# Attention among the experts' matmuls: a unit in two groups of steps, and single steps where attention is alone

## The chip, the cores and the metric

The kernel runs on one core of one Trainium2 chip. The metric is the device time of one execution in microseconds (us). It was 879.05 us in the median of three runs (876.48 to 881.49).

A core has five engines, each with its own queue of instructions: TensorE (PE in the profile; its weight loads are PEld), VectorE (DVE), ScalarE (ACT), GpSimd (POOL) and SyncE (SP). SP computes nothing here and issues most of the DMA transfers. An engine works through its queue in order, and an instruction waits until what it needs has been done by the other engines.

## The reference

Sigmoid attention over 8 batches, 12 heads, 448 rows and head size 64, and behind it a mixture of 8 experts on the 3584 x 768 result:

```python
scores = scale * np.matmul(q, k.transpose(0, 1, 3, 2)) - np.log(S)
attn = 1.0 / (1.0 + np.exp(-scores))
attn_out = np.matmul(attn, v)
...
logits = x @ w_gate
expert_idx = np.argmax(logits, axis=1)
...
for e in range(E):
    mask = expert_idx == e
    xe = x[mask]
    h = np.maximum(xe @ w1[e], 0.0)
    out[mask] = gate_w[mask, None] * (h @ w2[e])
```

Each row goes to one expert only, and gate_w is the softmax probability of that expert. There is no row maximum or sum in the attention, so a block of keys can be worked through by itself.

## The kernel before

**Stages.** First attention runs alone on TensorE. Then attention and the experts run side by side: for each batch of 448 rows the expert that most of its rows chose is applied to all of them. In a tail the rows that chose another expert are gathered into work items and done again. The change touches the first two stages.

**Attention.** Heads go in pairs, 48 pairs g in all (6 per batch); two pairs make a unit u, and the keys of a unit are cut into ST = 7 steps of 64 keys. So there are N_ST = 168 steps, s = 7u + i. For a step, `scores(s)` (L515) gives for each of the two pairs a tile of 128 x 448 scores in PSUM (tag "sc", a ring of 4 tiles, so two steps; the gate's small products take turns in the same ring), followed by the sigmoid on ScalarE into a tile `at` in SBUF (`squash`, L507; a ring of 8, so four steps). `weighted(s)` (L526) multiplies the sigmoids by v and sums over the 7 steps of the unit in one PSUM tile per pair (tag "av", a ring of 2, so one unit). After the last step of a unit the sums are read three times: a copy xh by ScalarE (L543), the rest xl = sum - xh by VectorE (L544) and a transpose into xt by VectorE (L400). All these products are 64 x 64 matmuls in float32, four of them side by side on the quarters of the array; each shows as two records in the trace, so one step of scores, or of value sums, is 8 records.

**Experts.** `moe(b, wts)` (L192) is a generator that yields after every matmul of 128 x 128 by 448 columns. A batch has 288: eight blocks of 18 for the first layer (L208) and six of 24 for the second (L229). Their PSUM tiles have the tag "moe", a ring of 2. Weights arrive as raw float32 tiles (`wst`, a ring of 5) and are split into two parts: a cast on ScalarE (L143) and a subtraction on GpSimd (L144). `wts.ahead(n)` emits loads and splits up to part n. A block of the first layer ends with a Relu on ScalarE (L213) and a VectorE operation (L214).

**Order.** In these stages the order of the instructions on each engine is the program's (`manual_schedule`). The generator `attention()` (L560) walks s from 0 to 178 and yields twice per s; at each yield the loop at L639 puts 7 expert matmuls (MIX) into the program, from s = START = 36 on. Between the yields come, by i = s mod 7, transposes of the next unit's k and q on VectorE and loads (`READY`, L553: `turn`, `load_pair`, `load_values`), and the parts of the gate of a batch (`gate_a` to `gate_e`, at fixed s behind the batch's last unit). `load_pair` issues 8 DMAs per pair on SP (L445); `token_rows` stores xt to x_tok with four DMAs on SP (L408); `load_regs` reads the chosen expert on SP, and the loads of `wst` follow on SP.

Attention products stand at every even s: first the value sums of all steps before s (before s - 1 as long as s < START), stopping at the end of a unit, and then the scores of s and s + 1. With s < 36 there are no expert matmuls, and these groups follow one another on TensorE.

Of the kernel before, what the change touches and what calls it, by code (L numbers as in the profile page):

```python
# [10 lines left out]
F32 = mybir.dt.float32  # L11
# [8 lines left out]
P = 128  # L20
# [5 lines left out]
def tile_sigmoid_attention_top1_moe(  # L26
# [41 lines left out]
    ps_moe = ctx.enter_context(tc.tile_pool(name="ps_moe", bufs=2, space=bass.MemoryType.PSUM))  # L68
# [317 lines left out]
    def load_regs(b):  # L386
        ri = gate_out[b]
        regs[b] = nc.sync.value_load(ri[0:1, 0:1], min_val=0, max_val=E - 1)
# [5 lines left out]
    def token_block(g, pv):  # L394

        b, t = divmod(g, NP)
        n, t = divmod(t, KH)
        if t == 0:
            xts[b, n] = xtpool.tile([P, S // 32, KH, 32], F32, tag="xt", bufs=2, name=f"xt_{b}_{n}")
        nc.vector.transpose(xts[b, n][:, :, t, :], pv.rearrange("p (j s) -> p j s", s=32))  # L400
        if t == KH - 1:
            turned.append((b, n))
# [18 lines left out]
    ps_av = att.enter_context(tc.tile_pool(name="ps_av", bufs=2, space=bass.MemoryType.PSUM))  # L421
# [10 lines left out]
    def quarter(g, h):  # L432

        return OWN[h if g % 2 == 0 else 1 - h]

    def load_pair(g):
        if g >= NG:
            return
        b, hp = divmod(g, NP)
        for nm, src in (("k", k), ("q", q)):  # L440
            t = apool.tile([P, S // 32, 32], F32, tag=nm + "n", bufs=4, name=f"{nm}n_{g}")
            for h in range(2):
                for f in range(D // 32):
                    a = 2 * h + f
                    nc.sync.dma_start(  # L445
                        t[32 * a : 32 * (a + 1)],
                        src[b, 2 * hp + h, :, 32 * f : 32 * (f + 1)].rearrange("(j r) s -> r j s", r=32),
                    )
            ops[g, nm + "n"] = t

    def first_pair(g):

        b, hp = divmod(g, NP)
        t = wpool.tile([P, 1024], F32, tag="wst", bufs=RAWS_AHEAD, name=f"first_{g}")
        tv = t[:PF].rearrange("p (n c h d) -> p n c h d", n=2, c=4, h=2)
        for n, src in enumerate((k, q)):
            for h in range(2):
                eng = nc.scalar if n else nc.sync
                eng.dma_start(tv[:, n, :, h], src[b, 2 * hp + h].rearrange("(p c) d -> p c d", c=4))
        ops[g, "first"] = t  # L460

    def first_turn(g):

        t = ops.pop((g, "first"))
        for n, nm in enumerate("kq"):
            ps = score_tile(f"first_{g}_{nm}")
            for c in range(4):
                at = (4 * n + c) * P
                nc.tensor.transpose(ps[:, c * PF : (c + 1) * PF], t[:PF, at : at + P], ident[:PF, :PF])
            to = apool.tile([P, S], F32, tag=nm + "t", bufs=4, name=f"{nm}t_{g}")  # L470
            tov, psv_ = to.rearrange("d (p c) -> d c p", c=4), ps[:, :S].rearrange("d (c p) -> d c p", c=4)
            if nm == "k":
                nc.vector.tensor_copy(tov, psv_)
            else:
                nc.scalar.copy(tov, psv_)
            ops[g, nm] = to

    def load_values(g):
        if g >= NG:
            return  # L480
        b, hp = divmod(g, NP)
        eng = nc.gpsimd if g < V_POOL else nc.sync
        t = apool.tile([P, KC, D], F32, tag="vn", bufs=4, name=f"vn_{g}")
        for h in range(2):
            eng.dma_start(t[quarter(g, h)], v[b, 2 * hp + h].rearrange("(p c) d -> p c d", c=KC))
        ops[g, "v"] = t
# [9 lines left out]
    def warm_up(n):  # L496

        ps = ps_moe.tile([P, 512], F32, tag="moe", name="ps_warm")
        for _ in range(n):
            nc.tensor.matmul(ps[:, :P], ones, ones, start=True, stop=True)  # L500

    ats, psv = {}, {}

    ST = KC
    N_ST = NG // 2 * ST

    def squash(g, c, ps):  # L507
        at = apool.tile([P, S], F32, tag="at", bufs=8, name=f"at_{g}_{c}")
        nc.scalar.activation(at, ps[:, :S], AF.Sigmoid, bias=bias_s, scale=SCALE)  # L509
        ats[g, c] = at  # L510

    def score_tile(name):
        return ps_sc.tile([P, 512], F32, tag="sc", name=f"sc_{name}")

    def scores(s):  # L515
        u, c = divmod(s, ST)
        two = [2 * u + n for n in range(2)]
        pss = [score_tile(f"{g}_{c}") for g in two]
        for g, ps in zip(two, pss):
            for h in range(2):  # L520
                ks = ops[g, "k"][OWN[h]].rearrange("d (p c) -> d c p", c=KC)[:, c]
                nc.tensor.matmul(ps[quarter(g, h), :S], ks, ops[g, "q"][OWN[h]], start=True, stop=True)  # L522
        for g, ps in zip(two, pss):
            squash(g, c, ps)

    def weighted(s):  # L526
        u, c = divmod(s, ST)
        two = [2 * u + n for n in range(2)]
        for g in two:
            if c == 0:  # L530
                psv[g] = ps_av.tile([P, 512], F32, tag="av", name=f"av_{g}")
            at = ats.pop((g, c))
            for h in range(2):
                rows = quarter(g, h)
                nc.tensor.matmul(  # L535
                    psv[g][OWN[h], :S], ops[g, "v"][rows, c, :], at[rows], start=(c == 0), stop=(c == KC - 1)
                )
        if c == KC - 1:
            for g in two:
                pv = psv.pop(g)  # L540
                xh = xpool.tile([P, S], F32R, tag="xh", name=f"xh_{g}")
                xl = xpool.tile([P, S], F32R, tag="xl", name=f"xl_{g}")
                nc.scalar.copy(xh, pv[:, :S])  # L543
                nc.vector.tensor_sub(xl, pv[:, :S], xh.bitcast(F32))  # L544
                token_block(g, pv[:, :S])
                xch[divmod(g, NP)] = (xh, xl)

    WARM, V_POOL = 50, 10
    START = 36
    PB = NP // 2 * ST  # L550
    MIX = (7, 7)

# [7 lines left out]
    def attention():  # L560

        order = ExitStack()
        order.enter_context(tc.manual_schedule())
        for g in range(2):
            first_pair(g)
        warm_up(WARM)
        for g in range(2):
            first_turn(g)
            load_values(g)
        for g in (2, 3):  # L570
            load_pair(g)
        nc.gpsimd.dma_start(wg, w_gate.rearrange("(t p) e -> p t e", p=P))
        pend_gate = None
        done_av = 0
        for s in range(N_ST + 11):
            u, i = divmod(s, ST)
            if s == 6:
                setup()
            if s == START - 1:
                wts.ahead(2)  # L580
            if s % 2 == 0:


                while done_av < min(s - (s < START), N_ST):
                    weighted(done_av)
                    done_av += 1
                    if done_av % ST == 0:
                        break
                for n in range(s, min(s + 2, N_ST)):
                    scores(n)  # L590
            yield s, MIX[0]
            if i in READY and s < N_ST:
                READY[i](u)
            gb = s - PB
            if gb >= 0:
                b, r = divmod(gb, PB)
                r -= 3 if b == 0 else 2
                at = ("a", "b", None, "c", "l", None, "d", None, "e")
                what = at[r] if 0 <= r < len(at) else None
                if what == "a":  # L600
                    gate_a(b)
                elif what == "b":
                    pend_gate = gate_b(b)
                elif what == "c":
                    pend_gate = gate_c(b, *pend_gate)
                    gate_out[b] = pend_gate[0]
                elif what == "l":
                    load_regs(b)
                    if b == 0:
                        wts.ahead(0)  # L610
                elif what == "d":
                    gate_d(b, *pend_gate)
                elif what == "e":
                    gate_e(b)
            yield s, MIX[1]
            if s % 2 == 0:
                while turned:
                    token_rows(*turned.pop(0))
        order.close()
# [19 lines left out]
    for s, n in attention():  # L639
        if s >= START:  # L640
            more(n)
# [304 lines left out]
```

## Time and profile before

| | |
|---|---|
| median of three runs | 879.05 us (876.48 to 881.49) |
| the profiled execution | 879.22 us, span 877.2 us |
| granted TensorE clock, mean | 0.994 |
| first attention product | 10.75 us |
| first expert matmul | 80.37 us |
| the last attention product is done | 701.2 us |
| HBM traffic | 97.55 MB read, 24.64 MB written |

The span reaches from the first to the last instruction of one profiled execution; the 2 us beside it lie around the program. In a row of the timeline stand the start and the length in us, the engine, the line of the kernel, the operation, output<-input, sizes and, behind x, how many instructions were merged into the row. In brackets stands how long the engine was idle before, and what released it. Rows that overlap run side by side.

### The profile page before, as it was taken

What the parts mean: (1) busy time and instruction counts of PE and PEld (TensorE: products, weight loads), DVE (VectorE), ACT (ScalarE), POOL (GpSimd) and SP (SyncE); (2) the same over time, 40 slices, a digit from 0 to 9 for tenths busy, and PEclk for the clock granted to TensorE, in tenths of its full rate; (3) what the DMA queues carried; (4) which work ended last, traced back from release to release, by engine and by line L of the source; (5) the groups of instructions that cost most, each with busy time, mean ns of one, the idle gap of its engine ahead of it and who ended that gap; (6) DMA issues with size and microseconds to landing.
All of it is one profiled execution on the core that took longest, in us unless ns stands there. A gap on an engine that the chain in (4) does not pass through costs nothing.

```text
span 877.2 us, 15559 instructions
## 1 busy us (share of the span) xinstructions
PE 851.8 (97%) x5612; PEld 627.8 (72%) x5612; DVE 298.2 (34%) x679; ACT 383.6 (44%) x691; POOL 410.1 (47%) x377
## 2 busy tenths in 40 slices
PE   8999999999999999999999999999999998999986
PEld 6545667677677667677667667677767687899775
DVE  2444135132332134122432135123332045426454
ACT  5766443444344444345344445255344421324444
POOL 4114234734275324834276324824285458766240
PEclk9999999999999999999999999999999999999999
DMA  8988874576457764675357654586253425556623
GB/s 146 147 146 185 178 164 116 131 163 140 98 115 148 170 141 107 148 155 142 64 138 179 158 117 100 125 190 146 57 135 111 133 52 145 146 159 192 211 65 134
DMA packets 301930, 120.61 MB, mean 137 GB/s; under 512 B 211588, under 2 KB 296660, under 8 KB 301856
## 3 DMA queue, kind: packets, MB, share of 16 engines
q1 hardware_dynamic: 292512, 104.25, 51.0%
q0 software_dynamic: 7488, 14.93, 7.0%
q8 instruction: 44, 0.72, 0.4%
q10 hardware_dynamic: 1856, 0.46, 0.3%
q14 instruction: 30, 0.25, 0.1%
HBM read 97.55 MB, written 24.64 MB: 139 GB/s over the span
## 4 chain that ended last, share of the span: by engine, by line
PE 83%; SPq 7%; issue 3%; POOL 2%; DMA 2%; DVE 1%; ACT 0%; POOLq 0%; ACTq 0%; DVEq 0%
PE ps L208 28%; PE ps L229 25%; PE av L535 12%; PE sc L522 11%; SPq L445 5%; PE ps L822 4%; PE psg L256 2%; DMA out_dram<-ob 1%; SPq L408 1%; DMA first<-in_q_dram 1%; POOL w1l L144 1%; DVE w1l_item L144 1%; POOL recs L361 0%; SPq L165 0%; POOL out_dram L244 0%
## 5 line engine op out<-in xcount | busy, mean ns | idle before, releaser
L509 ACT ACTIVATE at<-sc,bias_s 128x448 f32<-128x448 f32 x336 | 187.8, 641 | 219.6 <-PE sc L522 215.1
L144 POOL TENSOR_TENSOR w2l<-wst,w2h 128x512 fp32r<-128x512 f32 x96 | 121.6, 1291 | 172.6 <-ACT w2h L143 166.9
L144 POOL TENSOR_TENSOR w1l<-wst,w1h 128x768 fp32r<-128x768 f32 x64 | 116.8, 1840 | 130.2 <-ACT w1h L143 126.8
L535 PE MATMUL av<-at,vn 64*64 64x448 f32 x1344 | 156.4, 548 | 1.3 <-PE sc L522 0.7
L522 PE MATMUL sc<-qt,kt 64*64 64x448 f32 x1344 | 153.9, 540 | 0.0
L208 PE MATMUL ps<-xh,w1l 128*128 128x448 f32 x384 | 142.6, 371 | 5.5 <-POOL w1l L144 5.5
L229 PE MATMUL ps<-hh,w2l 128*128 128x448 f32 x384 | 143.1, 373 | 0.3 <-POOL w2l L144 0.3
L208 PE MATMUL ps<-xl,w1h 128*128 128x448 f32 x384 | 142.6, 371 | 0.0
L208 PE MATMUL ps<-xh,w1h 128*128 128x448 f32 x384 | 142.3, 371 | 0.0
L229 PE MATMUL ps<-hh,w2h 128*128 128x448 f32 x384 | 142.1, 370 | 0.0
L229 PE MATMUL ps<-hl,w2h 128*128 128x448 f32 x384 | 141.9, 370 | 0.0
L522 PEld LDWEIGHTS sc<-qt,kt 64*64 64x64 f32 x1344 | 77.8, 190 | 60.0 <-issue 51.0
L214 DVE SCALAR_TENSOR_TENSOR hl<-ps,hh 128x448 fp32r<-128x448 f32 x64 | 39.9, 624 | 209.5 <-ACT hh L213 209.5
L535 PEld LDWEIGHTS av<-at,vn 64*64 64x64 f32 x1344 | 48.4, 132 | 66.7 <-issue 51.7
L208 PEld LDWEIGHTS ps<-xh,w1l 128*128 128x128 f32 x384 | 72.6, 189 | 20.6 <-POOL w1l L144 8.6
L229 PEld LDWEIGHTS ps<-hh,w2l 128*128 128x128 f32 x384 | 74.6, 194 | 11.3 <-issue 5.8
L208 PEld LDWEIGHTS ps<-xl,w1h 128*128 128x128 f32 x384 | 72.5, 189 | 13.8 <-issue 8.0
L208 PEld LDWEIGHTS ps<-xh,w1h 128*128 128x128 f32 x384 | 72.6, 189 | 13.5 <-issue 7.2
L229 PEld LDWEIGHTS ps<-hh,w2h 128*128 128x128 f32 x384 | 74.6, 194 | 10.4 <-issue 6.5
L213 ACT ACTIVATE hh<-ps 128x448 fp32r<-128x448 f32 x64 | 35.3, 551 | 106.8 <-PE ps L208 106.8
L229 PEld LDWEIGHTS ps<-hl,w2h 128*128 128x128 f32 x384 | 74.6, 194 | 10.0 <-issue 6.5
L143 ACT CAST w2h<-wst 128x512 fp32r<-128x512 f32 x96 | 57.8, 627 | 50.2 <-PE ps L229 41.8
(150 smaller groups left out, 815.4 us busy)
## 6 DMA issues: line engine op xcount, KB each, us to landing
wst<-in_moe_w_dram SPq DMA_DIRECT2D x64, 384.0 KB
wst<-in_moe_w_dram SPq DMA_DIRECT2D x48, 512.0 KB
x_tok<-xt SPq DMA_DIRECT2D x64, 168.0 KB
out_dram<-ob POOLq DMA_DIRECT2D x96, 112.0 KB, 2.7
kn<-in_k_dram SPq DMA_DIRECT2D x184, 56.0 KB
qn<-in_q_dram SPq DMA_DIRECT2D x184, 56.0 KB
vn<-in_v_dram SPq DMA_DIRECT2D x76, 112.0 KB
w1r<-in_moe_w_dram SPq DMA_DIRECT2D x12, 512.0 KB
```

What stands on the lines that cost most here:

```text
L143: nc.scalar.copy(hi, st)
L144: eng.tensor_tensor(lo, st, hi.bitcast(F32), op=ALU.subtract)
L208: nc.tensor.matmul(ps[:, :S], a[:, ws], b_, start=(t == 0 and n == 0), stop=(t == KD - 1 and n == 2))
L213: nc.scalar.activation(hh[:, :S], ps[:, :S], AF.Relu)
L214: nc.vector.scalar_tensor_tensor(hl[:, :S], ps[:, :S], 0.0, hh[:, :S].bitcast(F32), op0=ALU.max, op1=ALU.subtract)
L229: nc.tensor.matmul(ps[:, :S], a, b_, start=(j == 0 and n == 0), stop=(j == KF - 1 and n == 2))
L256: nc.tensor.matmul(psg[: 2 * E, :S], wgs[:, t], xch[b, t][n], start=(t == 0 and n == 0), stop=(t == KD - 1 and n == 1),)
L445: nc.sync.dma_start(t[32 * a : 32 * (a + 1)], src[b, 2 * hp + h, :, 32 * f : 32 * (f + 1)].rearrange("(j r) s -> r j s", r=32),)
L509: nc.scalar.activation(at, ps[:, :S], AF.Sigmoid, bias=bias_s, scale=SCALE)
L522: nc.tensor.matmul(ps[quarter(g, h), :S], ks, ops[g, "q"][OWN[h]], start=True, stop=True)
L535: nc.tensor.matmul(psv[g][OWN[h], :S], ops[g, "v"][rows, c, :], at[rows], start=(c == 0), stop=(c == KC - 1))
L822: nc.tensor.matmul(*a, **kw)
```

## The change

Three things change in `attention()` and one in `weighted()`.

- For s < ALONE = 35 the steps go singly: the scores of s, then the value sums of s - 2.
- From s = 35 on attention products stand only at i = 0 and i = 4 of a unit. At i = 0: the scores of four steps, with the value sums of the three steps left from the unit before in between (scores, values, scores, values, scores, values, scores). At i = 4: one step of value sums first, then the scores of three steps with a step of value sums behind each.
- The value sums of units 1 and 3 (odd units, as long as attention is alone) are taken in the two PSUM tiles of the experts, tag "moe".
- `token_rows` runs at i = 1 and i = 5 instead of at every even s.

```diff
@@ weighted
         for g in two:
             if c == 0:
-                psv[g] = ps_av.tile([P, 512], F32, tag="av", name=f"av_{g}")
+                pool, tag = (ps_av, "av") if u % 2 == 0 or s >= ALONE else (ps_moe, "moe")
+                psv[g] = pool.tile([P, 512], F32, tag=tag, name=f"av_{g}")
             at = ats.pop((g, c))
...
     START = 36
+    ALONE = 35
@@ attention
         done_av = 0
+
+        def values(to):
+            nonlocal done_av
+            while done_av < min(to, N_ST):
+                weighted(done_av)
+                done_av += 1
+                yield
+
+        def steps(first, n, to):
+
+            vs = values(to)
+            for m in range(first, min(first + n, N_ST)):
+                scores(m)
+                next(vs, None)
+            for _ in vs:
+                pass
+
         for s in range(N_ST + 11):
             u, i = divmod(s, ST)
             if s == 6:
                 setup()
             if s == START - 1:
                 wts.ahead(2)
-            if s % 2 == 0:
-
-
-                while done_av < min(s - (s < START), N_ST):
-                    weighted(done_av)
-                    done_av += 1
-                    if done_av % ST == 0:
-                        break
-                for n in range(s, min(s + 2, N_ST)):
-                    scores(n)
+            if s < ALONE:
+                steps(s, 1, s - 1)
+            elif i == 0:
+                steps(s, 4, s)
+            elif i == 4:
+                for _ in zip(range(1), values(s)):
+                    pass
+                steps(s, 3, s)
             yield s, MIX[0]
...
             yield s, MIX[1]
-            if s % 2 == 0:
+            if i in (1, 5):
                 while turned:
                     token_rows(*turned.pop(0))
```

## The prediction

> **What bounds the kernel now.** I read the page first, for the engine and the chain that ended last.
>
> ```profile
> PE 851.8 (97%) x5612; PEld 627.8 (72%) x5612; DVE 298.2 (34%) x679; ACT 383.6 (44%) x691; POOL 410.1 (47%) x377
> ...
> PE 83%; SPq 7%; issue 3%; POOL 2%; DMA 2%; DVE 1%; ACT 0%; POOLq 0%; ACTq 0%; DVEq 0%
> ```
>
> TensorE (PE) is busy 97% of the span and 83% of the chain; next comes SP's issuing of loads (SPq). A share of busy time says nothing of single stages, so I cut the span at the first expert matmul (80.37 us) and behind the last attention product (701.20) and asked for busy time by stretch.
>
> ```profile
> 10.75:80.37 69.62, 67.03 (x606) 34.09 (x606) 28.07 (x73) 47.03 (x86) 12.71 (x23) 0.98 0.87 155
> 80.37:701.20 620.83, 619.93 (x4080) 444.79 (x4078) 186.45 (x453) 272.21 (x498) 297.74 (x251) 1.00 0.59 135
> 701.20:877.20 176.00, 157.24 (x867) 141.98 (x863) 80.60 (x144) 61.94 (x106) 92.47 (x82) 0.98 0.45 138
> ```
>
> The columns are length, then busy us of PE, PE's weight loads, VectorE (DVE), ScalarE (ACT) and POOL, the granted clock, the DMA share and GB/s. Three stages: attention alone, 69.6 us, with the DMA engines at 0.87; the mixed stage, 620.8 us, PE busy throughout at full clock; and a tail that the change doesn't touch. In the mixed stage only the time that PE takes per piece of work can shrink, so I read its timeline around one visit to the attention products.
>
> ```profile
> 303.18 0.36 PE L208 MATMUL ps<-xh,w1l 128*128 128x448 f32 x1
> 303.47 1.74 PE L535 MATMUL av<-at,vn 64*64 64x448 f32 x16
> 305.03 1.68 PE L522 MATMUL sc<-qt,kt 64*64 64x448 f32 x16
> 306.64 0.47 PE L208 MATMUL ps<-xh,w1h 128*128 128x448 f32 x1
> 306.95 0.36 PE L208 MATMUL ps<-xl,w1h 128*128 128x448 f32 x1
> ...
> 312.21 0.36 PE L208 MATMUL ps<-xh,w1h 128*128 128x448 f32 x1
> ```
>
> Expert matmuls start every 0.202 us (26 of them from 306.95 to 312.21). A step's scores or value sums are 8 records on four 64x64 tiles at a time. From the matmul at 303.18 to the second one behind the visit are 3.77 us. What should they be? In the stage of attention alone scores and values follow each other without a gap:
>
> ```profile
> 30.83 1.66 PE L522 MATMUL sc<-qt,kt 64*64 64x448 f32 x12
> ...
> 32.33 1.66 PE L535 MATMUL av<-at,vn 64*64 64x448 f32 x12
> ...
> 33.83 1.66 PE L522 MATMUL sc<-qt,kt 64*64 64x448 f32 x12
> ```
>
> Two steps of scores and two of values, so two changes between the kinds, take 3.00 us: 0.75 for one step of one kind. The visit then needs 4 x 0.75 + 2 x 0.20 = 3.41 us and took 3.77: **0.36 us are lost at each visit**. A larger visit, with three steps of values and two of scores, loses the same: 4.53 - 0.41 - 3.75 = 0.37.
>
> ```profile
> 284.36 0.37 PE L208 MATMUL ps<-xh,w1h 128*128 128x448 f32 x1
> 284.66 2.49 PE L535 MATMUL av<-at,vn 64*64 64x448 f32 x24
> 286.97 1.68 PE L522 MATMUL sc<-qt,kt 64*64 64x448 f32 x16
> ...
> 288.89 0.36 PE L208 MATMUL ps<-xh,w1l 128*128 128x448 f32 x1
> ```
>
> So the loss goes with the number of visits, not with the work in them. The stage's sum supports it: 1848 expert matmuls x 0.202 = 373, 263 steps x 0.75 = 197, 66 visits x 0.36 = 24 and six gates at about 3.2 (twelve matmuls and some small ones) = 19 give 613 of 620.8. PE's waits between 78 and 700 us are almost nothing:
>
> ```profile
> PE ps L208 <- POOL w1l L144: 0.6, 1, 0.6
> PE ps L229 <- POOL w2l L144: 0.3, 1, 0.3
> ```
>
> **The change, part by part.** *Fewer visits.* Before, attention enters at every even s; with expert matmuls on both sides that is s = 38 to 168, 66 visits, the last ended by this matmul:
>
> ```profile
> 701.20 0.47 PE L208 MATMUL ps<-xh,w1h 128*128 128x448 f32 x1
> ```
>
> After, it enters at i = 0 and i = 4 of a unit: s = 39, 42, 46 and on to 168, 38 visits. 28 x 0.36 = **10.1 us less**. The same number of expert matmuls stands between the same values of s, and the scores and values are the same.
>
> *What waits inside a larger visit.* Four score tiles hold two steps, so the third step of scores must wait until ScalarE has done the first's sigmoids; before, a visit had two steps and never met that.
>
> ```profile
> 90.39 2.21 ACT L509 ACTIVATE at<-sc,bias_s 128x448 f32<-128x448 f32 x4 [3.93 <-PE sc L522]
> 92.96 0.55 ACT L213 ACTIVATE hh<-ps 128x448 fp32r<-128x448 f32 x1 [0.36 <-PE ps L208]
> 93.40 0.82 ACT L143 CAST w1h<-wst 128x768 fp32r<-128x768 f32 x1
> ```
>
> Four sigmoids take 2.21 us, so 1.1 for a step, against 1.5 for PE's step with its values: ScalarE keeps up once it has begun. Scores 0 end 0.75 us into the visit, its sigmoids by about 2.2, and scores 2 are due at 3.0: 0.8 of slack. What can eat it is a Relu and a cast queued ahead (0.55 + 0.82 = 1.4), which holds the sigmoids until 1.4 to 1.6 if a block of expert matmuls ends just before the visit: still in time. Behind a waiting score stand only PE's own values and the next expert matmuls. The unit's two copies xh (about 1.0, quoted below) come before the last step's sigmoids, so ScalarE ends some 2 us behind PE; expert matmuls follow there for 56 or 42 x 0.2 us. Bounds: nothing, and 0.34 us in each of the 38 visits (a backlog of 2 us) = 13. I take 1 us, next to the rows, by which the slack holds.
>
> [...]
>
> *Attention alone, steps singly and odd units in the experts' banks.* The stage loses PE time at unit ends:
>
> ```profile
> 36.09 2.24 PE L522 MATMUL sc<-qt,kt 64*64 64x448 f32 x14
> 38.98 3.16 PE L535 MATMUL av<-at,vn 64*64 64x448 f32 x22 [0.66 <-PE sc L522]
> ```
>
> ```profile
> 37.13 0.98 ACT L543 CAST xh<-av 128x448 fp32r<-128x448 f32 x2
> ```
>
> ```profile
> 39.32 0.63 DVE L400 STREAM_TRANSPOSE xt<-av 128x448 f32<-128x448 f32 x1
> ```
>
> The next unit's values start at 38.98, as VectorE's reads of the old banks end. With other banks for odd units this wait goes. The work up to the first expert matmul is 38 steps of scores and 35 of values = 54.8 us, with the first gate's 3.4 (twelve matmuls from 54.03 to 56.5, below, and small ones) 58.2; the stage takes 69.6, so 11.4 us are lost. After, one step of scores more is done by then (35 to 38 in the first group), 59.0 us.
>
> ```profile
> 54.03 0.38 PE L256 MATMUL psg<-xh,wgs 128*16 128x448 f32 x1
> ...
> 56.29 0.37 PE L256 MATMUL psg<-xl,wgs 128*16 128x448 f32 x1
> ```
>
> How much comes back is set by what is late next, the loads. Unit 1's last turned q stands only at 21.7, and PE in its best order would want it at 19.8, so 1.9 us stay:
>
> ```profile
> 21.06 0.65 DVE L493 STREAM_TRANSPOSE qt<-qn 128x448 f32<-128x448 f32 x1 [1.38 <-DMA qn<-in_q_dram]
> ...
> 31.57 0.65 DVE L493 STREAM_TRANSPOSE qt<-qn 128x448 f32<-128x448 f32 x1 [2.14 <-DMA qn<-in_q_dram]
> ```
>
> Without further waits the first expert matmul could start at 10.75 + 59.0 + 1.9 = 71.7. But SP issues loads back to back, half a microsecond each, and the experts' first weights stand behind them:
>
> ```profile
> 30.69 1.99 SPq L445 DMA_DIRECT2D qn<-in_q_dram  x4
> 32.78 1.99 SPq L445 DMA_DIRECT2D kn<-in_k_dram  x4
> ...
> 68.86 4.11 SPq L165 DMA_DIRECT2D wst<-in_moe_w_dram  x5
> ```
>
> Nothing on SP before 67 us waits for PE, and the diff keeps the order of SP's queue there (the rows of x_tok go at i = 1, between the same loads). So the weights are issued at 68.9 again. A load lands some 2 us behind its last issue (32.68 to the transpose at 34.6 in the timeline; that of 384 KB estimated 2 to 3): 71.2.
>
> ```profile
> 78.85 1.57 ACT L143 CAST w1h<-wst 128x768 fp32r<-128x768 f32 x2
> ```
>
> These two casts now stand ahead of the sigmoids of step 35, and scores 37 and 38 wait for sigmoids 35 and 36: 71.2 + 1.57 + 2.3 + 0.2 + 0.9 = 76.2. In the trace the experts begin here:
>
> ```profile
> 80.37 0.47 PE L208 MATMUL ps<-xh,w1h 128*128 128x448 f32 x1
> ```
>
> So 80.4 - 76.2 + 0.75 (the extra step) = **4.9 us less**; bounds 0 and 80.4 - 71.7 + 0.75 = 9.4.
>
> [...] In this trace the issues are back to back, which speaks for SP.
>
> *Moves without a price.* Storing x_tok at i = 1 and 5 instead of even s puts it later behind the evictions, never ahead of a load it used to follow by more than a step; it waits less on SP, and in the mixed stage SP mostly waits for free weight buffers. Values of a unit now begin at i = 4, when the old banks have been empty for 11 us; if that cover went, the price would be the 2 to 3 us per unit seen above.
>
> *Sum.* - 10.1 + 1.0 - 4.9 = -14. The profiled execution took 879.22 us (span 877.2), next to the median of 879.05; so **865 us**, own range 862 to 869.
>
> **Rivals.** *A. Attention alone gains nothing*, since loads hold it (DMA share 0.87, SP back to back) and the casts come first: 879.2 - 10.1 + 1.0 = 870. Against it: waits at unit ends are on PE's banks. *B. SP doesn't hold it*: 879.2 - 10.1 - 9.4 + 1.0 = 861. Against it the SP rows. *C. ScalarE breaks up the larger visits*, so that the change doesn't do what it says: with 0.34 us in 19 to 38 visits, 6.5 to 13, the time is 871 to 877; the 0.8 us of slack is against it. *D. Slower: changing between scores and values costs PE time beside expert matmuls.* Before, a visit has one change, 65 in all; after, six in each, 222: 157 more. In the visit above 16 value records take 1.56 us to the scores' start instead of 1.50; at 0.06 a change this is +9, 874. If half of the 0.36 belongs to the change, it is +28 while the visits save only 5: 898. Beyond 19/157 = 0.12 us a change the kernel is slower by over 0.5%. Against it: the 3.00 us above hold two changes at no cost; for it only that alternation beside full-size matmuls isn't in the trace.
>
> **How the numbers follow.** Forecast 55%, A 15%, B 8%, C 14%, D 8%. The range 860 to 872 holds the forecast, A, B and the near half of C; 15% is left out. A measurement of this kernel tells about 0.5%, 4.4 us, from no change. Faster by more (below 874.8): forecast, A, B and half of C, 85%; within: 6 of C, 3 of D, 9%; slower: 1 of C, 5 of D, 6%.
>
> **What would show it.** In the timeline: 38 visits, each of 7 steps' halves in 5.25 + 0.36 us; first expert matmul near 76; attention's last product ending near 687; the tail as long as before. A gap before the third scores with ScalarE as releaser is C; a visit longer than 6.1 us without a wait is D; a first expert matmul at 80 is A, at 72 B. Weights that come late in the longer runs of expert matmuls (11 us instead of 6), seen as PE waiting for POOL, would make all of it wrong.

## The result and the profile after

The changed kernel takes 887.05 us (median of four runs, 887.02 to 887.83) against 878.16 for the kernel before in the same comparison: a ratio of 1.0088, 95% interval 1.0065 to 1.011. It is **slower by 0.9%**, where 865 us was forecast, with a range of 860 to 872. The profiled execution took 887.08 us with a span of 885.1. Times and ratios here and below leave out a few executions in a slow state (one of e7's six, for example, took 1441 us at a granted clock of 0.64).

The same cut into three stages, now at the first expert matmul (81.87 us) and behind the last attention product (709.17); columns as before:

```profile
11.28:81.87 70.59, 66.75 (x615) 43.34 (x614) 28.69 (x75) 51.20 (x92) 15.67 (x24) 0.94 0.84 152
81.87:709.17 627.30, 615.07 (x4072) 451.70 (x4070) 187.49 (x452) 276.34 (x491) 294.98 (x249) 0.99 0.58 134
709.17:885.10 175.93, 158.52 (x867) 143.00 (x863) 80.83 (x144) 62.01 (x106) 92.51 (x82) 0.97 0.44 137
```

The tail is as long as before (176). Attention alone ends 1.5 us later, though it then has one step of scores more behind it (0.75); this is less than executions of one program differ by, for in the profile of e5 below, whose first stage is that of the changed kernel, the experts start at 79.70. The mixed stage, where 10 us were to be saved, is 6.5 us longer. PE was busy for 619.9 of 620.8 us there; now it is idle for 12 of 627, and the granted clock has fallen to 0.99. The waits of PE, in the page's list of who waited for whom, say for what:

```profile
PE ps L229 <- POOL w2l L144: 12.2, 4, 3.6
PE ps L208 <- POOL w1l L144: 4.8, 2, 3.8
PE sc L522 <- ACT at L509: 2.5, 1, 2.5
```

The second row is the tail's (4.9 before). The first is new: four waits for the low parts of the second layer's weights, which GpSimd (POOL) makes; before it was one of 0.3. One of the four in PE's timeline:

```profile
449.02 0.37 PE L229 MATMUL ps<-hl,w2h 128*128 128x448 f32 x1
453.03 0.47 PE L229 MATMUL ps<-hh,w2l 128*128 128x448 f32 x1 [3.65 <-POOL w2l L144]
453.35 0.29 PE L381 MATMUL pg<-gm,same 128*128 128x16 f32 x2
453.49 0.60 PE L229 MATMUL ps<-hh,w2h 128*128 128x448 f32 x1
453.89 0.57 PE L229 MATMUL ps<-hl,w2h 128*128 128x448 f32 x1
...
455.75 0.57 PE L229 MATMUL ps<-hh,w2h 128*128 128x448 f32 x1
456.26 1.35 PE L536 MATMUL av<-at,vn 64*64 64x448 f32 x8
```

4.0 us from one start to the next, 3.65 of them idle, and behind it matmuls start every 0.37 us instead of 0.20. The granted clock (third figure from the end) is halved for 3.41 us there:

```profile
453.64:457.05 3.41, 3.41 (x11) 2.16 (x15) 0.82 (x2) 0.00 (x0) 3.41 (x3) 0.50 0.48 132
```

So this wait of 3.65 us is paid for again, in a clock of 0.50 for 3.41 us. What does GpSimd do in the meantime?

```profile
439.97 0.15 POOL L357 IOTA rec<- 128x4 uint32 x1
446.75 1.04 POOL L361 DMA_INDIRECT recs<-rec,si  x1 [6.62 <-issue]
448.10 1.02 POOL L361 DMA_INDIRECT recs<-rec,si  x1 [0.30 <-issue]
449.42 0.98 POOL L361 DMA_INDIRECT recs<-rec,si  x1 [0.31 <-issue]
450.71 0.98 POOL L361 DMA_INDIRECT recs<-rec,si  x1 [0.30 <-issue]
451.70 3.73 POOL L144 TENSOR_TENSOR w2l<-wst,w2h 128x512 fp32r<-128x512 f32 x3
```

It stands at the gate's four scatters (`gate_d`): first it waits for their row numbers, which VectorE (L355) has written by 445.87, then it issues them for 5 us, and the three splits in its queue come behind. The cast that the first of these splits needs was done at 444.45 (a row of ScalarE's timeline: start 443.83, 0.62 us). GpSimd's timeline at the same place in the kernel before, and PE's under it:

```profile
447.76 1.04 POOL L361 DMA_INDIRECT recs<-rec,si  x1 [3.45 <-issue]
449.12 1.02 POOL L361 DMA_INDIRECT recs<-rec,si  x1 [0.30 <-issue]
450.44 0.98 POOL L361 DMA_INDIRECT recs<-rec,si  x1 [0.30 <-issue]
451.73 0.98 POOL L361 DMA_INDIRECT recs<-rec,si  x1 [0.30 <-issue]
452.72 3.77 POOL L144 TENSOR_TENSOR w2l<-wst,w2h 128x512 fp32r<-128x512 f32 x3
```

```profile
444.60 0.19 PE L340 MATMUL pr<-lm,upper 128*128 128x32 bf16 x1
...
446.28 1.73 PE L535 MATMUL av<-at,vn 64*64 64x448 f32 x16
447.83 1.68 PE L522 MATMUL sc<-qt,kt 64*64 64x448 f32 x16
...
454.08 0.48 PE L229 MATMUL ps<-hh,w2l 128*128 128x448 f32 x1 [0.28 <-POOL w2l L144]
```

GpSimd was no faster: from PE's product pr, with which the gate's last part starts, to the splits it took 8.1 us (444.60 to 452.72), and 8.1 after (443.58 to 451.70). But a visit to attention lay between, 3.4 us in which PE used no expert weights, and with it GpSimd was late by 0.28 us only. The change moved that visit behind the place where the weights are needed.

### The profile page after: what moved, and what is told of

Read it like the earlier page. It is cut to its first block, busy times and chain, and to the rows that moved or that the text cites. A ratio compares the mean times of both kernels' runs of the same rounds, so it can differ in the third digit from the quotient of the medians.

```text
span 885.1 us, 15521 instructions
## 1 busy us (share of the span) xinstructions
PE 848.2 (96%) x5612; PEld 645.1 (73%) x5612; DVE 300.1 (34%) x679; ACT 392.0 (44%) x691; POOL 410.3 (46%) x377
## 4 chain that ended last, share of the span: by engine, by line
PE 83%; issue 4%; DMA 4%; POOL 3%; DVE 2%; SPq 2%; ACT 1%; POOLq 0%; ACTq 0%; DVEq 0%
PE ps L208 27%; PE ps L229 23%; PE sc L522 13%; PE av L536 13%; PE ps L839 3%; PE psg L256 2%; POOL recs L361 1%; SPq L445 1%; DMA w2r<-in_moe_w_dram 1%; DMA first<-in_q_dram 1%; POOL w2l L144 1%; DMA out_dram<-ob 1%; DVE w1l_item L144 1%; SPq L408 1%; DMA wst<-in_moe_w_dram 0%
## 5 line engine op out<-in xcount | busy, mean ns | idle before, releaser
L509 ACT ACTIVATE at<-sc,bias_s 128x448 f32<-128x448 f32 x336 | 196.0, 636 | 198.8 <-PE sc L522 198.6
L522 PE MATMUL sc<-qt,kt 64*64 64x448 f32 x1344 | 177.0, 556 | 3.3 <-ACT at L509 2.5
L536 PE MATMUL av<-at,vn 64*64 64x448 f32 x1344 | 172.5, 544 | 0.0
L229 PE MATMUL ps<-hh,w2l 128*128 128x448 f32 x384 | 144.5, 376 | 12.2 <-POOL w2l L144 12.2
L536 PEld LDWEIGHTS av<-at,vn 64*64 64x64 f32 x1344 | 55.6, 134 | 57.4 <-issue 55.1
```

The costliest lines, as they stand in the source:

```text
L229: nc.tensor.matmul(ps[:, :S], a, b_, start=(j == 0 and n == 0), stop=(j == KF - 1 and n == 2))
L536: nc.tensor.matmul(psv[g][OWN[h], :S], ops[g, "v"][rows, c, :], at[rows], start=(c == 0), stop=(c == KC - 1))
```

## The experiments

Theory 1: the scatters stand ahead of the splits in GpSimd's queue, and the visit that covered them is gone from there. Theory 2: longer runs of expert matmuls use weights up faster than loads and splits bring them, wherever the scatters stand. Rivals for smaller parts were that the loss comes from the first stage, and that larger visits cost more than thought. Each kernel was timed against the kernel before on its own chip, which took 881 to 882 us there, so the ratios are to be compared.

**e1: the scatters ahead of a visit.** In the changed kernel two parts of the gate change places; the scatters come 28 expert matmuls later, and a visit follows 7 behind them.

```diff
-                at = ("a", "b", None, "c", "l", None, "d", None, "e")
+                at = ("a", "b", None, "c", "l", None, "e", None, "d")
```

> The changed kernel (887 us) with two parts of the gate exchanged: gate_e at the place of gate_d, and gate_d (with its four scatters on GpSimd) two steps of s later, so that a visit to the attention products follows 7 expert matmuls behind it. Theory 1, the scatters stand ahead of three splits in GpSimd's queue and the longer run of expert matmuls reaches the split weights before GpSimd does: the waits of PE for w2l (12.2 us in four places) and the slow clock behind them (about 4 us) go, 870 to 873 us, and the visits stay at 38. Theory 2, the longer runs use weights up faster than loads and splits bring them, wherever the scatters stand: the waits stay or move, 883 to 889 us.

Measured: 872.24 us, ratio 0.9886 (0.9864 to 0.9907), so 1.1% faster than the kernel before. The mixed stage takes 609.4 us (81.61 to 691.04), with no wait of PE in it. GpSimd's timeline behind the same gate:

```profile
442.26 1.28 POOL L144 TENSOR_TENSOR w2l<-wst,w2h 128x512 fp32r<-128x512 f32 x1 [4.57 <-ACT w2h L143]
443.71 2.53 POOL L144 TENSOR_TENSOR w2l<-wst,w2h 128x512 fp32r<-128x512 f32 x2 [0.16 <-ACT w2h L143]
...
453.07 1.05 POOL L361 DMA_INDIRECT recs<-rec,si  x1 [0.28 <-POOL rec L357]
```

The splits are done at 446.2, before the first scatter at 453.07. Theory 2 falls: the runs of expert matmuls are as long as in the changed kernel, and loads and splits keep up. In its tail this kernel's profile loses 3.7 us (870.7 - 691.0 = 179.7 against 176.0). The last batch's scatters come later there too, but that they are the cause is not shown: the tail of e3 below, where they stand as before, takes 179.4.

**e2: only the two groups per unit.** Attention alone goes as before, in the old banks and with `token_rows` at its old place (the lines for these two are left out here), and from s = 35 on as in the changed kernel.

```diff
...
             if s < ALONE:
-                steps(s, 1, s - 1)
+                if s % 2 == 0:
+                    while done_av < s - 1:
+                        weighted(done_av)
+                        done_av += 1
+                        if done_av % ST == 0:
+                            break
+                    for n in range(s, min(s + 2, ALONE)):
+                        scores(n)
...
```

> Only the two groups per unit from s = 35 on; attention alone goes as in the kernel before (two steps at a time, the old banks). Theory 1 (the loss is in the mixed stage, 18 us of waits and slow clock against 9 us of saved visits): 884 to 888 us, PE waiting for w2l about 12 us again. Rival, the loss comes from the first stage, whose first expert matmul came 1.5 us later: 870 to 872 us.

Measured: 889.69 us, ratio 1.0102 (1.0063 to 1.014), with the same four waits, 12.2 us in all. The loss belongs to the mixed stage, not to the first.

**e3: only the single steps and the banks.** The groups from s = 36 on are those of the kernel before.

```diff
-            if s < ALONE:
+            if s < START:
                 steps(s, 1, s - 1)
-            elif i == 0:
-                steps(s, 4, s)
...
+            elif s % 2 == 0:
+                while done_av < min(s, N_ST):
...
```

> Only the single steps and the experts' banks while attention is alone; from s = 36 on as in the kernel before (visits at every even s). Theory 1: PE does the steps without gaps until about 74 us but then waits for the experts' weights, so the first expert matmul stays near 80 us and the time near the kernel before, 876 to 880 us; no waits of PE for w2l beyond 0.5 us. Rival (the forecast's term): 4.9 us less, 873 to 875 us.

Measured: 879.53 us, ratio 0.9984 (0.9964 to 1.0005): no difference that can be told. In its profile the first expert matmul starts at 77.71 us instead of 80.37, and PE has waited for sigmoids just before:

```profile
76.23 1.55 PE L522 MATMUL sc<-qt,kt 64*64 64x448 f32 x8 [1.07 <-ACT at L509]
77.71 0.47 PE L208 MATMUL ps<-xh,w1h 128*128 128x448 f32 x1
```

The loads went out at 69.78. So up to 2.7 us may be in it, in one execution; the timed runs show 1.4 us, with an interval that takes in no change, and in the profile the tail is 3.4 us longer than before (179.4).

**e4: the first casts behind the group.** In the changed kernel `wts.ahead(2)` moves behind the products of s = 35.

```diff
-            if s == START - 1:
-                wts.ahead(2)
             if s < ALONE:
...
+            if s == START - 1:
+                wts.ahead(2)
             yield s, MIX[0]
```

> The changed kernel (887 us) with the first two splits of expert weights put behind the group of s = 35 instead of ahead of it. If PE's 2.5 us of waiting for sigmoids there come from the casts that wait for the weights' landing ahead of them in ScalarE's queue, that wait goes and the first expert matmul comes at 78 to 79 us instead of 81.9: 884 us. If the sigmoids themselves hold PE, it stays at 887.

Measured: 893.14 us, ratio 1.0123 (1.0098 to 1.0147), no better than the changed kernel (1.0088; the intervals overlap). The wait for sigmoids did go and the first expert matmul came at 79.84, but the casts then stood behind eight sigmoids and two copies, and PE waited there instead:

```profile
79.84 0.74 PE L208 MATMUL ps<-xh,w1h 128*128 128x448 f32 x1 [2.66 <-ACT w1h L143]
80.38 0.57 PE L208 MATMUL ps<-xl,w1h 128*128 128x448 f32 x1
81.74 0.74 PE L208 MATMUL ps<-xh,w1l 128*128 128x448 f32 x1 [0.79 <-POOL w1l L144]
```

Stage by stage, this is the clock:

```profile
80.00:90.00 10.00, 9.21 (x33) 7.77 (x34) 1.18 (x2) 2.51 (x4) 6.60 (x4) 0.69 1.01 180
```

Ten us at a granted clock of 0.69, against 0.92 in the changed kernel's same stretch. The expected wait went, but the time did not fall: one wait was exchanged for another.

**e5: without the scatters.** The changed kernel, with gate_d's four scatters left out for batches 1 to 6; the rest of the gate stays.

```diff
-        for c in range(NCH):
+        for c in range(NCH if b in (0, 7) else 0):
             put = nc.gpsimd.indirect_dma_start(
                 out=recs,
```

> The changed kernel without the four scatters of gate_d for batches 1 to 6; the rest of the gate is left as it is. The records of those batches are not written, so the rows that chose another expert there are not done again. If the scatters themselves (about 5.3 us of GpSimd ahead of the splits) make PE wait in the mixed stage, the waits for w2l (12.2 us) go and the mixed stage falls from 627 to about 610 us; the whole about 870 us. If the waits came from GpSimd's idle time before them (VectorE's chain) or from late loads, a part of 2 us or more per place stays.

Measured: 866.58 us, ratio 0.9837 (0.9817 to 0.9857), and no wait of PE between 80 and 689 us. The mixed stage takes 609.1 us (79.70 to 688.81), 18.2 less than the changed kernel's 627.3. **Of these 18.2 the waits are 12.2, and 6 us are left for the slow clock behind them.** Matmul for matmul against e5, 1.8 us are lost behind each of the three long waits, beside the wait itself, and 0.3 behind the shortest: 5.7 in all. Without the scatters VectorE's chain doesn't hold GpSimd's queue either, so e5 removes the wait for the row numbers with them. The split of the delay is in the rows above: from the cast at 444.45 to the splits at 451.70 are 7.25 us, of which 2.3 are before the first scatter and 5 the scatters.

**e6: the first weights earlier on SP.** In the changed kernel the chosen expert of batch 0 is read, and the first five loads of its weights are issued, ahead of the loads of pair 12.

```diff
+            if s == PB + 7:
+                load_regs(0)
+                wts.ahead(0)
             if i in READY and s < N_ST:
                 READY[i](u)
...
-                elif what == "l":
+                elif what == "l" and b > 0:
                     load_regs(b)
-                    if b == 0:
-                        wts.ahead(0)
```

> The changed kernel (887 us) with the first five loads of expert weights put ahead of the loads of pair 12 in SP's queue (8 loads, about 5 us). If SP's order holds the first expert matmul, as the forecast had it, the loads go out near 67 us instead of 72, PE no longer waits for sigmoids behind the casts, and the first expert matmul comes at 77 to 78 instead of 81.9: 882 to 883 us. Rival, ScalarE and the ring of score tiles hold it: it stays within 1 us of 887.

Measured: 884.4 us, ratio 1.0037 (1.0017 to 1.0057). The loads go out at 65.39, PE doesn't wait, and the experts start 4.9 us sooner than in the changed kernel, 1 us of it because the first product already came sooner (10.30 against 11.28):

```profile
74.46 2.60 PE L522 MATMUL sc<-qt,kt 64*64 64x448 f32 x16
76.99 0.47 PE L208 MATMUL ps<-xh,w1h 128*128 128x448 f32 x1
```

Against e5, whose loads went out at 70.39 and whose experts started at 79.70, they start 2.7 us sooner. So SP's order did hold the start. By the ratios the gain over the changed kernel is 0.5%, some 4.5 us, and the intervals don't overlap.

**e7: both.** Early weights, and the exchange of e1 for all batches but the last.

```diff
-                at = ("a", "b", None, "c", "l", None, "d", None, "e")
+                at = ("a", "b", None, "c", "l", None) + (("e", None, "d") if b < B - 1 else ("d", None, "e"))
```

> Early weights and the exchange of gate_d and gate_e together, the exchange for batches 0 to 6 only (for the last batch it made the tail 3.7 us longer). If the two causes are separate, the gains add: mixed stage 609 us, first expert matmul at 77 to 78, tail 176: 864 to 867 us of device time, about 2% below the kernel before.

Measured: **865.46 us, ratio 0.9825 (0.9808 to 0.9842)**, 1.75% faster than the kernel before and the fastest complete kernel here. Its stages:

```profile
10.88:77.83 66.95, 64.52 (x614) 32.98 (x613) 27.82 (x74) 50.80 (x90) 14.55 (x24) 1.00 0.85 153
77.83:686.95 609.12, 609.12 (x4072) 449.75 (x4071) 197.96 (x454) 277.08 (x493) 296.00 (x250) 1.00 0.61 139
686.95:865.50 178.55, 158.72 (x867) 143.02 (x863) 80.64 (x144) 61.85 (x106) 92.33 (x82) 0.97 0.44 135
```

In the mixed stage PE is busy for all of 609.12 us: 11.7 less than before (620.83), of which 0.75 is the step of scores that now comes earlier. The tail is 2.5 us longer than before in this profile, and from 807.18 on the granted clock in it is 0.50 for 3.41 us; what sets this off was not followed up.

**e8: the exchange without the change.** The kernel before, with gate_d and gate_e exchanged for batches 0 to 6 by the line of e7.

> The kernel before with gate_d and gate_e exchanged for batches 0 to 6. If the exchange is worth something only where a longer run of expert matmuls follows the scatters, the time stays within 2 us of the kernel before (its wait of PE for w2l is 0.3 us in all). If the exchange is a gain by itself: 868 to 872.

Measured: 881.62 us, ratio 1.0012 (0.9989 to 1.0034). The exchange is worth nothing by itself; it pays back what the change uncovered.

## Why the prediction was wrong

*Fewer visits: right.* There are 38, and several steps of scores and values in turn cost nothing extra. One that starts with scores, in the changed kernel:

```profile
501.69 0.37 PE L208 MATMUL ps<-xh,w1l 128*128 128x448 f32 x1
501.99 1.04 PE L522 MATMUL sc<-qt,kt 64*64 64x448 f32 x8
502.86 0.93 PE L536 MATMUL av<-at,vn 64*64 64x448 f32 x8
...
507.47 0.47 PE L208 MATMUL ps<-xh,w1h 128*128 128x448 f32 x1
507.78 0.36 PE L208 MATMUL ps<-xl,w1h 128*128 128x448 f32 x1
```

6.09 us, less 0.41 for two expert matmuls and 5.25 for seven half steps, leave 0.43, with six changes between scores and values inside where a visit before had one; a visit of seven half steps that starts with values loses 0.36 to 0.38. The forecast's 10.1 us is nearly borne out by e5 and e7: their mixed stages are 11 us shorter than before, the extra step taken off. Of these 11, 0.9 are the two short waits of the kernel before (0.6 and 0.3), and 8.6 come out of a count of the visits (66 x 0.36 - 20 x 0.37 - 18 x 0.43); the rest has no place yet. With that rival D, a cost of changing between scores and values, falls, though the time came out on its side of the kernel before: right sign, another mechanism.

*Inside a larger visit: right.* ScalarE kept pace: PE's waits between 80 and 709 us are the four for w2l, 12.2 us, and there is none for sigmoids, so rival C has nothing to show here.

*The step that failed* is that the sum puts the longer runs of expert matmuls, between the visits, at nothing. Its only price for waits, 1 us, weighs what waits inside a visit and ends there: "expert matmuls follow there for 56 or 42 x 0.2 us" was said for ScalarE's sake, and what those runs need from GpSimd was put into the last sentence, without a price. It measured 18.2 us in four places. The sign was in a row that the prediction quotes as almost nothing, PE's wait of 0.3 us for w2l: it is the place at 454.08 above, where a visit's 3.4 us had just been used up as cover. A wait near nothing was read as slack, when it was the end of it. Four of the six gates in this stage are hit because the position of gate_d within the expert's blocks moves by 6 matmuls per batch. For the gates of batches 3 to 6 it stands between matmul 23 of the third block of the second layer and matmul 17 of the fourth. The last one to three splits stand behind it, and the first of them is due 27 to 33 matmuls later, ahead of the next visit, which comes after 35. For the gates of batches 1 and 2 it stands 12 and 6 matmuls earlier; the first split is due after 45 and 39, so the visit still lies between, and PE does not wait. (The positions are worked out from the program's order and agree with the trace.)

*Attention alone: right in kind, and it gained nothing that can be told (e3).* The waits at unit ends did go (PE runs single steps of 1.5 us without a gap, busy for all 33 us from 17 to 50), and SP was the next bound, as written. But the 4.9 us needed weights at 68.9 and landed at 71.2; they were issued at 71.92 and landed at 75.6:

```profile
75.59 0.83 ACT L143 CAST w1h<-wst 128x768 fp32r<-128x768 f32 x1 [2.24 <-DMA wst<-in_moe_w_dram]
76.96 0.83 ACT L143 CAST w1h<-wst 128x768 fp32r<-128x768 f32 x1 [0.54 <-DMA wst<-in_moe_w_dram]
77.70 2.21 ACT L509 ACTIVATE at<-sc,bias_s 128x448 f32<-128x448 f32 x4
```

So landing took 3.7 us, not 2.3 (the 2 to 3 us for 384 KB were an estimate that no run shows), and SP was 3 us later than before. With the order of the whole change and loads still in the old place (the changed kernel, e1, e4, e5) they went out at 70.4 to 71.9, against 68.3 to 69.1 where attention alone goes as before (the kernel before, e2, e8) and 69.8 in e3. Why SP is slower beside single steps is not settled; its own waits in the list are some tenths of a us each. Rival A, no gain at 870 us, came nearest for this stage, and e6 shows the cause that it named for loads.

*The sum.* The span grew by 7.9 us: 1.5 in the first stage; in the mixed stage - 0.75 for the extra step, - 11.0 for the visits and the two short waits (e5 against the kernel before) and + 18.2 for the splits and the clock; - 0.1 in the tail. With the splits' wait and the late weights taken away, e7 takes the forecast's 865, in part by luck: in its profile the mixed stage gains 11.0 where 9.1 were forecast, the experts start at 77.83 and not at 76.2, and the tail is 2.5 us longer.

## What to carry to other kernels

Work that is moved away from a place was covering something there: before its waits are counted as gone, follow every in-order queue over the new, longer stretch and ask what stands ahead of the next thing needed. A wait of a few tenths of a us in a tight pipeline can mark where cover has just run out, as the one of 0.28 us did here. And when two streams are regrouped, move the rare long piece of a helper engine (here four scatters, 5 us) to the place where the regrouping has put the cover.

## What the runs showed that was not expected

In these runs a wait of PE could cost more than its length. In the changed kernel, behind the waits of 3.34 to 3.65 us matmuls started every 0.37 us until the next visit; behind the one of 1.89 us they didn't:

```profile
350.75 0.37 PE L229 MATMUL ps<-hl,w2h 128*128 128x448 f32 x1
353.01 0.47 PE L229 MATMUL ps<-hh,w2l 128*128 128x448 f32 x1 [1.89 <-POOL w2l L144]
353.32 0.37 PE L229 MATMUL ps<-hh,w2h 128*128 128x448 f32 x1
```

The next matmul comes 0.31 us later, as behind a visit (507.47 to 507.78 above). Length alone does not decide, though. In e2 the same wait (1.87 us, up to 354.16) was followed by half the clock. The views, of e2 and then of the changed kernel, have the length, the busy us of PE and, third from the end, the granted clock:

```profile
351.55:354.96 3.41, 1.54 (x10) 0.85 (x12) 0.69 (x3) 0.00 (x0) 3.11 (x3) 1.00 0.02 3
354.96:358.37 3.41, 3.41 (x20) 1.07 (x20) 0.00 (x0) 0.38 (x1) 3.23 (x3) 0.50 0.52 154
```

```profile
351.24:354.65 3.41, 1.64 (x14) 0.94 (x18) 0.00 (x0) 0.00 (x0) 3.39 (x4) 1.00 0.09 25
354.65:358.06 3.41, 3.41 (x40) 1.60 (x36) 0.00 (x0) 2.27 (x4) 3.12 (x4) 1.00 0.70 200
```

The three slow stretches in the changed kernel's mixed stage last 3.41 us each, from 453.64, 556.04 and 658.44. In the 3.41 us ahead of them PE was idle for 2.80, 2.80 and 2.72 us; in the first view of e2 it was idle for 1.87, and in that of the changed kernel, behind which the clock stayed at 1.00, for 1.77. Twelve waits took 3.33 to 3.65 us, three each in the changed kernel, e2, e4 and e6, and behind every one of them matmuls came to start every 0.37 us. Of the four of 1.87 to 1.89, those in e2 and e4 were followed by attention products at half the pace (one step's every 1.5 us instead of 0.75), those in the changed kernel and e6 were not; what decides is not settled by these runs. In the changed kernel the slow clock turned 12.2 us of waiting into 18.2.
